# Attention in three units of 384 tokens instead of two batches of 576, with wider loads and first-matrix chunks cut by rows

## The chip, the cores and the metric

The kernel runs on one core of a Trainium2 chip. A core has five engines that run their own instruction queues in order and wait for each other by semaphores: TensorE (PE; its weight loads are listed as PEld), VectorE (DVE), ScalarE (ACT), GpSimd (POOL) and SyncE (SP), which here only issues transfers. The metric is the device time of one execution in microseconds. The kernel before took 690.56 us (median of 3 runs, 688.92 to 690.76).

## The reference

Local attention over 2 batches, 8 heads, 576 tokens and 64 columns a head, then two feed-forward blocks on the 1152 tokens of 512 columns:

```python
mask_plain = (rel >= 0) & (rel < 32)                          # heads 0 to 3
mask_dil = (rel >= 0) & (rel < 128) & (rel % 4 == 0)          # heads 4 to 7
scores = np.where(masks, scale * q @ k.T, -1e9)
attn = exp(scores - max); attn = attn / (sum + 1e-9)
x = (attn @ v), heads side by side                            # [1152, 512]

for e in range(4):                                            # experts, F = 1024
    out += p[:, e:e + 1] * (np.maximum(x @ w1[e], 0.0) @ w2[e])

h = out @ w_in                                                # 512 x 2048, float64
return (h - np.tanh(h)) @ w_out
```

`p` are the row-normalised domain probabilities. The second block's matrices come as float64.

## The kernel before, in words

**Feed-forward part.** The 1152 tokens are three groups g of 384 (T). The hidden columns are cut into 12 slices s of 512: 8 for the four experts, 4 for the tanh block. For one (s, g) there are seven *steps*: four h steps (`h_step`, 48 matmuls of 128x384, then a Relu or tanh on ACT and a subtraction on DVE that splits the result into a high and a low part) and three y steps (`y_step`, 36 matmuls of 128x512 and one eviction). Every product is three matmuls: high x high, high x low, low x high. Slices 0 and 1 are taken group by group, (0,0), (1,0), (0,1), (1,1), (0,2), (1,2); from slice 2 on each slice runs over all three groups.

**Weights.** A slice's weights are four chunks: c = 0, 1 from the first matrix, c = 2, 3 from the second. `w_load` fetches a chunk into one of three raw buffers; `w_split` copies it to the high part `whi` on ACT and writes the low part `wlo` on POOL (or DVE, for two of slice 0's chunks). Before, chunk c of the first matrix holds 256 hidden columns of all 512 rows. Slice 1's chunks are loaded at steps 0 to 3 and split at steps 1 to 4. In the tanh block `w_decode` on DVE first turns float64 into float32, in tiles of the tag "pn" of pool sp.

**Attention.** Two batches b; in each, a `Plain` object (heads 0 to 3) and a `Dilated` one (heads 4 to 7), each of two *pairs* of heads: pairs n = 0 to 3. A `Pair` has stages in *slots* 2n + lag: `scores` (PE, lag 0), `largest` of head a (mask, maximum on DVE, subtraction on POOL, lag 1 + a), `exps` (ACT, 1 + a), `norm` (sum and reciprocal on DVE, multiply on POOL, 2 + a), `p_transposes` (PE and a copy on ACT, 3 + a), `values` (PE, lag 5, then the high part of x on ACT and the low part on DVE). Scores of a head fill 5 stacks of 128 x 96. Within a slot the order is largest, norm, values, transposes, exps, early matmuls, splits, scores, loads. Values take two PSUM banks of pool "a" and transposes one or two; the pool has two banks.

**What sets the order.** All is written out by hand: each engine runs its instructions as the program emits them. Batch 0's 13 slots come first, with a few matmuls of step (0,0) put in as `early_h` when their x is there; then the steps run, and the table `beside` holds what is emitted after step i: loads, splits, decodes, and batch 1's slot t after step t (steps 0 to 12). Group 1 needs tokens of both batches. Transfers go through SP's queue alone, in the order of the program, and one that waits for a buffer holds those behind it.

Of the kernel before, what the change touches and what calls it, by code (L numbers as in the profile page):

```python
# [23 lines left out]
NST = 5  # L24
# [7 lines left out]
ROWS = S // DIL  # L32
CUTS = [(0, BQ), (BQ, BQ), (2 * BQ, ROWS - 2 * BQ)]

# [7 lines left out]
def _halves():  # L42


    out, at = [], [0, 0, 0]
    for b in range(2):
        for unit, plain in [((b, 0, ROWS), True)] + [((b, *cut), False) for cut in CUTS]:
            out.append((unit, plain, tuple(at)))
            nb, M, K = blocks(unit[2], plain)
            at[0] += 2 * nb * M  # L50
            at[1] += 2 * ((nb - 1) * (M if plain else K) + K)
            at[2] += nb * 4 * HEAD
    return out, at
# [6 lines left out]
def tile_local_attention_moe_tanhshrink(  # L60
# [30 lines left out]
    ld = ctx.enter_context(tc.tile_pool(name="ld", bufs=1))  # L91
# [14 lines left out]

    masks = {p: const.tile([128, NST, BK], F32, name=f"mask_{p}") for p in (True, False)}
# [5 lines left out]
    def emit_consts():  # L113

        mp, md = masks[True], masks[False]

        def band(out, m):
            nc.gpsimd.memset(out, 0.0)
            nc.gpsimd.affine_select(
                out=out, in_=out, pattern=[[1, BK]], base=-1, channel_multiplier=-1,  # L120
                compare_op=ALU.is_ge, fill=NEG,
            )
            nc.gpsimd.affine_select(
                out=out, in_=out, pattern=[[-1, BK]], base=HALO, channel_multiplier=1,
                compare_op=ALU.is_ge, fill=NEG,
            )

        def no_halo(out, in_):
            nc.gpsimd.affine_select(
                out=out, in_=in_, pattern=[[1, BK]], base=-HALO, channel_multiplier=0,  # L130
                compare_op=ALU.is_ge, fill=NEG,
            )

        for p in (0, BQ):
            band(mp[p:p + BQ, 1, :], BQ)
        no_halo(md[:, 0, :], mp[:, 1, :])
        nc.vector.tensor_copy(out=mp[:BQ, 0, :], in_=md[:BQ, 0, :])
        nc.vector.tensor_copy(out=mp[BQ:, 0, :], in_=mp[BQ:, 1, :])
        nc.vector.tensor_copy(
            out=mp[:, 2:, :], in_=mp[:, 1, :].unsqueeze(1).to_broadcast([128, NST - 2, BK])  # L140
        )
        make_identity(nc, ident)

    def emit_consts_dilated():
        mp, md = masks[True], masks[False]
        nc.gpsimd.tensor_copy(out=md[:, 1, :], in_=md[:, 0, :])
        nc.gpsimd.tensor_copy(out=md[:, 2:4, :], in_=mp[:, 1:3, :])
        for p in range(0, 128, 32):
            nc.vector.tensor_copy(out=md[p:p + 32, 4, :], in_=mp[:32, 1, :])
# [13 lines left out]
    class Plain:  # L163


        plain = True

        def __init__(self, b):
            self.b = b
            self.at = HALVES[b * (1 + len(CUTS))][2]  # L170
            self.q, self.k = {}, {}

        def load_qk(self, c):
            qo, ko, _ = self.at
            self.q[c] = ld.tile([128, S], F32, tag="q", name="pq", bufs=2)
            self.k[c] = ld.tile([128, S + HALO], F32, tag="k", name="pk", bufs=2)
            for src, o, n, dst in ((q, qo, S, self.q[c]), (k, ko, S + HALO, self.k[c])):
                nc.sync.dma_start(out=dst, in_=src[:, o + c * n:o + (c + 1) * n])

        def load_v(self):  # L180
            nb = S // BQ
            self.v = ld.tile([BK, nb, 4 * D], F32, tag="pv", name="pv")
            o = self.at[2]
            nc.sync.dma_start(
                out=self.v, in_=v[:BK, o:o + nb * 4 * D].rearrange("p (j f) -> p j f", j=nb)
            )

        def scores(self, c):

            out = []  # L190
            for j in range(2 * NST):
                o = min(j, S // BQ - 1) * BQ
                out.append((j % 2 * BQ, j // 2, self.q[c][:, o:o + BQ], self.k[c][:, o:o + BK]))
            return out

        def values(self):

            cut = S // BQ // 2
            return [
                (j, j * BQ, int(j >= cut), (j - cut * (j >= cut)) * BQ, BQ) for j in range(S // BQ)  # L200
            ]

        def spans(self, x):

            cut = S // BQ // 2 * BQ
            x = x[:, self.b * S:(self.b + 1) * S]
            return [(x[:, :cut], cut, None), (x[:, cut:], S - cut, None)]

    class Dilated:


        plain = False

        def __init__(self, b):
            self.b = b
            self.parts = HALVES[b * (1 + len(CUTS)) + 1:(b + 1) * (1 + len(CUTS))]
            self.q, self.k = {}, {}

        def load_qk(self, c):
            self.qat, self.kat, nq, nk = [], [], 0, 0  # L220
            for (_, _, W), _, _ in self.parts:
                self.qat.append(nq)
                self.kat.append(nk)
                nq, nk = nq + DIL * W, nk + DIL * (W + HALO)
            tail = BK - self.parts[-1][0][2] - HALO
            self.q[c] = ld.tile([128, S + 32], F32, tag="q", name="dq", bufs=2)
            self.k[c] = ld.tile([128, nk + tail], F32, tag="k", name="dk", bufs=2)
            nc.gpsimd.memset(self.q[c][:, nq:], 0.0)
            nc.gpsimd.memset(self.k[c][:, nk:], 0.0)
            for ((_, _, W), _, at), qo, ko in zip(self.parts, self.qat, self.kat):  # L230
                for src, o, n, dst, d in (
                    (q, at[0], DIL * W, self.q[c], qo),
                    (k, at[1], DIL * (W + HALO), self.k[c], ko),
                ):
                    nc.sync.dma_start(out=dst[:, d:d + n], in_=src[:, o + c * n:o + (c + 1) * n])  # L235

        def load_v(self):
            self.v = ld.tile([BK, DIL * len(CUTS), 4 * D], F32, tag="dv", name="dv")
            for u, (_, _, at) in enumerate(self.parts):
                n = DIL * 4 * D  # L240
                nc.sync.dma_start(
                    out=self.v[:, u * DIL:(u + 1) * DIL, :],
                    in_=v[:BK, at[2]:at[2] + n].rearrange("p (j f) -> p j f", j=DIL),
                )

        def scores(self, c):
            out = []
            for u, ((_, _, W), _, _) in enumerate(self.parts):
                for r in range(DIL):
                    o = self.qat[u] + r * W  # L250
                    w = self.kat[u] + r * (W + HALO)
                    full = W == BQ
                    out.append((
                        r % 2 * BQ if full else r * 32, 2 * u + r // 2 if full else NST - 1,
                        self.q[c][:, o:o + (BQ if full else 32)], self.k[c][:, w:w + BK],
                    ))
            return out

        def values(self):
            out = []  # L260
            for r in range(DIL):
                for u, ((_, p0, W), _, _) in enumerate(self.parts):
                    full = W == BQ
                    t = (2 * u + r // 2) * 128 + r % 2 * BQ if full else (NST - 1) * 128 + r * 32
                    out.append((u * DIL + r, t, r // 2, r % 2 * ROWS + p0, W))
            return out

        def spans(self, x):
            x = x[:, self.b * S:(self.b + 1) * S].rearrange("c (p r) -> c r p", r=DIL)
            return [(x[:, i:i + 2], 2 * ROWS, 2) for i in (0, 2)]  # L270

    class Pair:
# [7 lines left out]
        def scores(self):  # L280
            which = self.banks["s"]
            self.sb = [
                bank(which)[:, :NST * BK].rearrange("p (j c) -> p j c", c=BK) for _ in range(2)
            ]
            for part, j, qs, ks in self.h.scores(self.c):
                M = qs.shape[1]
                for a in range(2):
                    nc.tensor.matmul(  # L288
                        out=self.sb[a][part:part + M, j, :],
                        lhsT=qs[D * a:D * a + D, :], rhs=ks[D * a:D * a + D, :],  # L290
                        start=True, stop=True,
                    )

        def largest(self, a):
            s = sp.tile([128, 512], F32, tag="s", name="s")[:, :NST * BK].rearrange(
                "p (j c) -> p j c", c=BK
            )
            nc.vector.scalar_tensor_tensor(
# [453 lines left out]
```

## Time and profile before

| | us |
|---|---|
| median of 3 runs | 690.56 |
| the profiled execution | 689.82 |
| its span | 687.90 |
| TensorE busy | 652.1 (95%) |
| VectorE, ScalarE, GpSimd busy | 323.4, 205.1, 149.6 |

The span is the time from the first to the last instruction of the profile; the rest of the execution's time lies around it. The page's second part cuts the span into 40 slices of 17.2 us and gives the tenths of each that an engine was busy. TensorE's row begins 5767789 and is 9 from there to the last slice but one, so the idle time lies in the first seventh. The chain of work that ended last is 85% TensorE, and of it 40% in y steps and 42% in h steps.

### The profile page before, as it was taken

The page shows a single profiled execution, that of the slowest core. Times are in us where ns is not written, and L with a number is a line of the kernel's source. Part 1 is how long each engine was busy: PE and PEld are TensorE (multiplying, and loading weights), DVE is VectorE, ACT ScalarE, POOL GpSimd, SP SyncE. Part 2 cuts the span into 40 slices and gives each one's busy share as a digit, 9 for nine tenths or more (in the row PEclk, how much of TensorE's full clock was granted, in tenths as well). Part 3 has the DMA queues.
Part 4 walks back from the last instruction along what each step waited for, and adds up shares of the span by engine and source line. Part 5 has one row for each costly group of instructions (what it writes and reads, how often), then busy time and mean ns, then how long its engine had stood idle before and what let it go on. Part 6 is the DMA issues. An engine that isn't in the chain of part 4 may idle for free.

```text
span 687.9 us, 9361 instructions
## 1 busy us (share of the span) xinstructions
PE 652.1 (95%) x3839; PEld 580.4 (84%) x3839; DVE 323.4 (47%) x533; ACT 205.1 (30%) x376; POOL 149.6 (22%) x117
## 2 busy tenths in 40 slices
PE   5767789999999999999999999999999999999997
PEld 3556689999999999999999999888888888888886
DVE  6665442121222222222222222877687699698333
ACT  3453431214121121121121121333555443344221
POOL 4646410004221121121121121212022122122000
PEclk8698989999999999999999999999999999999999
DMA  9879100001221010010011021213133123220111
GB/s 250 222 142 263 31 1 1 1 0 55 70 68 55 31 61 32 31 61 31 31 61 31 31 62 30 92 61 92 38 100 98 47 96 94 70 99 7 47 46 46
DMA packets 27610, 46.23 MB, mean 67 GB/s; under 512 B 3504, under 2 KB 14512, under 8 KB 27376
## 3 DMA queue, kind: packets, MB, share of 16 engines
q1 hardware_dynamic: 27568, 45.64, 22.3%
q8 instruction: 30, 0.49, 0.3%
q14 instruction: 12, 0.10, 0.0%
HBM read 43.27 MB, written 2.36 MB: 66 GB/s over the span
## 4 chain that ended last, share of the span: by engine, by line
PE 85%; DVE 6%; DMA 3%; issue 2%; ACT 1%; POOL 1%; SPq 1%; DVEq 0%; POOLq 0%; ACTq 0%
PE bank_y L525 40%; PE bank_h L483 21%; PE bank_a L483 21%; DMA dk<-in_k_dram 2%; DMA raw<-in_moe_w_dram 1%; PE bank_a L335 1%; DVE t L433 1%; SPq L235 1%; POOL s L304 1%; PE bank_s L288 1%; DVE t L436 1%; DVE acc L537 1%; DVE t L429 1%; PE bank_y L670 1%; ACT h L494 1%
## 5 line engine op out<-in xcount | busy, mean ns | idle before, releaser
L525 PE MATMUL bank_y<-whi,h 128*128 128x512 f32 x864 | 277.5, 394 | 0.0
L525 PEld LDWEIGHTS bank_y<-whi,h 128*128 128x128 f32 x864 | 160.6, 188 | 39.1 <-DVE h L507 3.1
L525 PE MATMUL bank_y<-wlo,h 128*128 128x512 f32 x432 | 169.0, 391 | 0.0
L483 PE MATMUL bank_h<-x,whi 128*128 128x384 f32 x592 | 154.2, 341 | 0.0
L483 PE MATMUL bank_a<-x,whi 128*128 128x384 f32 x544 | 138.7, 335 | 2.6 <-DVE h L495 1.7
L459 POOL TENSOR_TENSOR wlo<-raw,whi 128x1024 fp32r<-128x1024 f32 x30 | 71.7, 2393 | 279.2 <-ACT whi L458 279.2
L483 PEld LDWEIGHTS bank_h<-x,whi 128*128 128x128 f32 x592 | 109.8, 192 | 3.0 <-issue 0.2
L483 PE MATMUL bank_h<-x,wlo 128*128 128x384 f32 x296 | 101.0, 341 | 0.0
L483 PEld LDWEIGHTS bank_a<-x,whi 128*128 128x128 f32 x544 | 98.0, 188 | 3.3 <-DVE h L495 2.2
L537 DVE SCALAR_TENSOR_TENSOR acc<-bank_y,pn,acc 128x512 f32<-128x512 f32 x63 | 47.1, 749 | 101.8 <-PE bank_y L525 101.8
L525 PEld LDWEIGHTS bank_y<-wlo,h 128*128 128x128 f32 x432 | 81.1, 188 | 15.4
L483 PE MATMUL bank_a<-x,wlo 128*128 128x384 f32 x272 | 90.9, 334 | 0.0
L494 ACT ACTIVATE h<-bank_h 128x384 fp32r<-128x384 f32 x50 | 24.5, 490 | 206.5 <-PE bank_h L483 206.5
L459 POOL TENSOR_TENSOR wlo<-t,whi 128x512 fp32r<-128x512 f32 x32 | 43.1, 1348 | 175.7 <-ACT whi L458 161.1
L495 DVE SCALAR_TENSOR_TENSOR h<-bank_h,h 128x384 fp32r<-128x384 f32 x50 | 27.8, 557 | 106.6 <-ACT h L494 106.6
L495 DVE SCALAR_TENSOR_TENSOR h<-bank_a,h 128x384 fp32r<-128x384 f32 x44 | 24.5, 558 | 69.0 <-ACT h L494 69.0
L483 PEld LDWEIGHTS bank_h<-x,wlo 128*128 128x128 f32 x296 | 56.8, 192 | 0.0
L483 PEld LDWEIGHTS bank_a<-x,wlo 128*128 128x128 f32 x272 | 51.1, 188 | 0.0
L494 ACT ACTIVATE h<-bank_a 128x384 fp32r<-128x384 f32 x44 | 21.6, 492 | 61.7 <-PE bank_a L483 61.7
L458 ACT ACTIVATE whi<-t 128x512 fp32r<-128x512 f32 x32 | 20.2, 630 | 57.8 <-DVE t L442 57.8
L458 ACT ACTIVATE whi<-raw 128x1024 fp32r<-128x1024 f32 x32 | 33.6, 1052 | 2.9 <-DMA raw<-in_moe_w_dram 2.9
L433 DVE SCALAR_TENSOR_TENSOR t<-raw,t 128x512 int32<-128x512 int32 x32 | 33.9, 1060 | 1.1
(163 smaller groups left out, 466.3 us busy)
## 6 DMA issues: line engine op xcount, KB each, us to landing
raw<-in_moe_w_dram SPq DMA_DIRECT2D x32, 512.0 KB, 3.6
raw<-in_moe_w_in_dram SPq DMA_DIRECT2D x16, 512.0 KB, 3.6
raw<-in_moe_w_out_dram SPq DMA_DIRECT2D x16, 512.0 KB, 3.3
dv<-in_v_dram SPq DMA_DIRECT2D x6, 384.0 KB, 8.2
out_dram<-oacc SPq DMA_DIRECT2D x8, 256.0 KB, 2.0
pv<-in_v_dram SPq DMA_DIRECT2D x2, 864.0 KB, 11.3
dk<-in_k_dram SPq DMA_DIRECT2D x8, 192.0 KB, 6.9
pk<-in_k_dram SPq DMA_DIRECT2D x4, 304.0 KB, 4.2
```

Of the source, the lines that this page charges most:

```text
L235: nc.sync.dma_start(out=dst[:, d:d + n], in_=src[:, o + c * n:o + (c + 1) * n])
L288: nc.tensor.matmul(out=self.sb[a][part:part + M, j, :], lhsT=qs[D * a:D * a + D, :], rhs=ks[D * a:D * a + D, :], start=True, stop=True,)
L304: nc.gpsimd.tensor_tensor(out=s, in0=s, in1=nm.unsqueeze(2).to_broadcast([128, NST, BK]), op=ALU.add)
L335: nc.tensor.transpose(pb[:BK, j * 128:(j + 1) * 128], self.p[a][:, j, :], ident)
L433: nc.vector.scalar_tensor_tensor(out=t, in0=high, scalar=-0x40000000, in1=t, op0=ALU.bitwise_and, op1=ALU.bitwise_or)
L458: nc.scalar.activation(out=hi, in_=raw, func=ACTF.Copy)
L459: (engine or nc.gpsimd).tensor_tensor(out=lo, in0=raw, in1=hi.bitcast(F32), op=ALU.subtract)
L483: nc.tensor.matmul(out=state["bank", f], lhsT=a, rhs=x[:, b_, :], start=(kk == 0 and n == 0), stop=(kk == KD - 1 and n == 2),)
L494: nc.scalar.activation(out=ht[:, 0, :], in_=hb, func=ACTF.Relu)
L495: nc.vector.scalar_tensor_tensor(out=ht[:, 1, :], in0=hb, scalar=0.0, in1=ht[:, 0, :].bitcast(F32), op0=ALU.max, op1=ALU.subtract,)
L525: nc.tensor.matmul(out=y, lhsT=a, rhs=b_, start=(f == 0 and n == 0), stop=(f == NF - 1 and n == 2),)
L537: nc.vector.scalar_tensor_tensor(out=acc[ch], in0=y, scalar=p, in1=acc[ch], op0=ALU.mult, op1=ALU.add)
```

## The change

Attention is cut by group instead of by batch: unit g holds the 384 tokens of group g (unit 1 is made of the end of batch 0 and the start of batch 1, two parts). Unit 0's slots come first; unit 1's slot t stands after step t and unit 2's slot t after step 14 + t, so that unit g is finished before group g's first step. A pair's scores are now 3 stacks of 96 (288 columns), or 4 of 80 (320) in unit 1's dilated pairs. Values take one PSUM bank and transposes one. Both pairs of a kind are loaded together, v on 128 partitions. The masks are small bf16 tiles for each unit, copied on DVE in slots 1, 9 and 10. Slice 0's splits stand in slots 4 (POOL), 7 (POOL), 9 (DVE) and 11 (POOL), before in slots 3 (DVE), 6 (POOL), 9 (DVE) and 11 (POOL). Slice 1's chunks are loaded at steps 0, 2, 4, 6 and split at steps 1, 3, 5, 7. A first-matrix chunk is 256 rows of all 512 columns, so every h step reads both chunks. The tag "pn" has two buffers, before three.

```diff
-ROWS = S // DIL
-CUTS = [(0, BQ), (BQ, BQ), (2 * BQ, ROWS - 2 * BQ)]
+UNITS = [[(0, 0, 96)], [(0, 96, 48), (1, 0, 48)], [(1, 48, 96)]]
...
+    def emit_mask(g, plain):
+        m = masks[g, plain]
+        copy = nc.vector.tensor_copy
+        if plain:
+            copy(out=cols(m, 0, 3), in_=wide(m_std, 3))
...
+        copy(out=cols(m, 0, 2), in_=wide(m_first if g == 0 else m_std, 2))
+        nc.vector.memset(m[:, 2 * BK:2 * BK + HALO], NEG)
         for p in range(0, 128, 32):
+            copy(out=m[p:p + 32, 2 * BK + HALO:3 * BK], in_=m_std[:32, :BQ])
...
         def values(self):
             h = self.h
-            xb = [bank(self.banks["x"]) for _ in range(2)]
-            for blk, t, i, o, n in h.values():
+            xb = bank(self.banks["x"])
+            for blk, keys, t, o, n in h.values():
...
+            (hi, src), (lo, _) = (h.order(xT[self.kk][:, j], xb) for j in range(2))
+            nc.scalar.activation(out=hi, in_=src, func=ACTF.Copy)
+            nc.vector.tensor_tensor(out=lo, in0=src, in1=hi.bitcast(F32), op=ALU.subtract)
...
-                dst = raw.rearrange("p (k f) -> p k f", k=KD)
-                src = a[:, c * 256:(c + 1) * 256].rearrange("(k p) f -> p k f", p=128)
+                dst = raw.rearrange("p (k f) -> p k f", k=2)
+                src = a[c * 256:(c + 1) * 256, :].rearrange("(k p) f -> p k f", p=128)
...
-        t = sp.tile([128, 512], F32, tag="pn", name="t", bufs=3).bitcast(I32)
+        t = sp.tile([128, 512], F32, tag="pn", name="t").bitcast(I32)
...
-        o = kk * 256 + (f % 2) * 128
-        return [t[:, o:o + 128] for t in wt[s, f // 2]]
+        o = kk % 2 * FV + f * 128
+        return [t[:, o:o + 128] for t in wt[s, kk // 2]]
...
+    for g in range(NG - 1):
+        put_load(g, 2, kinds[g + 1, True].load_qk)
+        put_load(g, 7, kinds[g + 1, True].load_v)
+        put_load(g, 6, kinds[g + 1, False].load_qk)
+        put_load(g, 11, kinds[g + 1, False].load_v)
+        put_load(g, 9, lambda g=g: emit_mask(g + 1, True))
+        put_load(g, 10, lambda g=g: emit_mask(g + 1, False))
+    put_load(0, 1, lambda: emit_mask(0, False))
...
-        (3, early[0], nc.vector), (6, early[1], nc.gpsimd), (9, early[2], nc.vector),
+        (4, early[0], nc.gpsimd), (7, early[1], nc.gpsimd), (9, early[2], nc.vector),
         (11, early[3], nc.gpsimd),
...
-        put(i, lambda sc=sc: w_load(*sc))
-        put(i + 1, lambda sc=sc: w_split(*sc))
+        put(2 * i, lambda sc=sc: w_load(*sc))
+        put(2 * i + 1, lambda sc=sc: w_split(*sc))
...
+    for g in range(1, NG):
+        for t, emits in enumerate(slots[g]):
+            for _, emit in sorted(emits, key=lambda e: e[0]):
+                put((g - 1) * 2 * PER + t, emit)
```

How the instructions stand in the queues, at three places. SP's queue at the start, before (pq, pk, pv are the plain heads' inputs, dq, dk, dv the dilated ones', raw a weight chunk):

```order
L178 DMA pq<-in_q_dram 128x576
L178 DMA pk<-in_k_dram 128x608
L178 DMA pq<-in_q_dram 128x576
L178 DMA pk<-in_k_dram 128x608
L418 DMA raw<-in_moe_w_dram 128x4x256
L184 DMA pv<-in_v_dram 96x2304
L418 DMA raw<-in_moe_w_dram 128x4x256
L235 DMA dq<-in_q_dram 128x256
L235 DMA dk<-in_k_dram 128x384
L235 DMA dq<-in_q_dram 128x256
L235 DMA dk<-in_k_dram 128x384
```

and after:

```order
L204 DMA q<-in_q_dram 128x384
L204 DMA k<-in_k_dram 128x416
L204 DMA q<-in_q_dram 128x384
L204 DMA k<-in_k_dram 128x416
L212 DMA v<-in_v_dram 128x1536
L204 DMA q<-in_q_dram 128x768
L204 DMA k<-in_k_dram 128x1024
L401 DMA raw<-in_moe_w_dram 128x2x512
L212 DMA v<-in_v_dram 128x1024
L401 DMA raw<-in_moe_w_dram 128x2x512 x2
```

The dilated pairs' q and k moved ahead of the first weight chunk, as two transfers for both pairs, and stand behind no buffer that has to come free.

POOL's queue in the first slots, before (s is the subtraction, pn__ the multiply of a head, wlo a split):

```order
L304 TENSOR_TENSOR s<-s,nm 128x480
L326 TENSOR_TENSOR pn__293<-p,rs 128x480
L304 TENSOR_TENSOR s<-s,nm 128x480
L326 TENSOR_TENSOR pn__349<-p,rs 128x480
L304 TENSOR_TENSOR s<-s,nm 128x480
L326 TENSOR_TENSOR pn__394<-p,rs 128x480
L459 TENSOR_TENSOR wlo<-raw,whi 128x1024
```

and after:

```order
L306 TENSOR_TENSOR s<-s,nm 128x288
L324 TENSOR_TENSOR pn__263<-p,rs 128x288
L449 TENSOR_TENSOR wlo<-raw,whi 128x1024
L306 TENSOR_TENSOR s<-s,nm 128x288
L324 TENSOR_TENSOR pn__307<-p,rs 128x288
L306 TENSOR_TENSOR s<-s,nm 128x288
L324 TENSOR_TENSOR pn__342<-p,rs 128x288
```

The first split on POOL moved from behind the fifth head's multiply (pn__394) to behind the third head's (pn__263).

TensorE's queue in a slot that holds values, beside the y steps, before (pt and last are the transposed weights of attention):

```order
L357 MATMUL bank_a<-pt,pv 64x64 x16
L357 MATMUL bank_a<-last,pv 64x64 x2
L335 MATMUL bank_a<-ident,pn__841 96x128 x4
L525 MATMUL bank_y<-whi,h 128x512
L525 MATMUL bank_y<-wlo,h 128x512
```

and after:

```order
L345 MATMUL bank_a<-pt,v 64x64 x12
L331 MATMUL bank_a<-ident,pn__692 96x128 x3
L515 MATMUL bank_y<-whi,h 128x512
L515 MATMUL bank_y<-wlo,h 128x512
```

The values' 18 matmuls into two banks became 12 into one; the transposes still stand right behind them.

## Rows read from the trace of the kernel before

**Rows 1.** Busy us by engine in four stretches; then clock, DMA share, GB/s.

```profile
0.00:43.90 43.90, 29.08 (x416) 21.11 (x416) 28.24 (x61) 19.46 (x34) 21.66 (x37) 0.81 0.88 220
43.90:109.53 65.63, 51.76 (x533) 44.58 (x533) 31.26 (x60) 23.33 (x43) 27.32 (x25) 0.90 0.32 91
109.53:142.62 33.09, 33.09 (x170) 30.20 (x169) 6.71 (x11) 6.01 (x11) 0.00 (x0) 1.00 0.00 1
142.62:687.90 545.28, 538.15 (x2725) 484.48 (x2723) 257.21 (x402) 156.28 (x288) 100.62 (x56) 1.00 0.18 56
```

**Rows 2.** The chain that ended last, 102 to 143 us (start us, us, what).

```profile
102.36 1.51 PE bank_a L357 x48
...
134.42 8.20 PE bank_y L525 x36
```

**Rows 3.** The same chain in the first 30 us.

```profile
4.83 1.06 PE bank_s L288 x40
...
7.30 11.29 DMA dk<-in_k_dram
...
19.65 0.67 PE bank_s L288 x16
...
27.84 1.26 PE bank_h L288 x48
```

**Rows 4.** TensorE's timeline, 52 to 85 us (in brackets: idle before, releaser).

```profile
52.85 1.87 PE L288 MATMUL bank_s<-pk,pq 64*64 64x96 f32 x38 [4.67 <-DVE s L298]
...
84.21 0.61 PE L335 MATMUL bank_a<-ident,pn__968 128*96 128x128 f32 x4 [3.00 <-DVE x L368]
```

**Rows 5.** Timeline of POOL and ACT, 47 to 55 us.

```profile
47.33 2.35 POOL L459 TENSOR_TENSOR wlo<-raw,whi 128x1024 fp32r<-128x1024 f32 x1 [1.23 <-ACT whi L458]
...
49.64 0.99 POOL L304 TENSOR_TENSOR s<-s,nm 128x480 f32<-128x480 f32 x1
...
51.17 0.47 ACT L494 ACTIVATE h<-bank_h 128x384 fp32r<-128x384 f32 x1
...
54.53 1.06 ACT L458 ACTIVATE whi<-raw 128x1024 fp32r<-128x1024 f32 x1 [2.89 <-DMA raw<-in_moe_w_dram]
```

**Rows 6.** Groups by line and form, 0 to 110 us (busy us, mean ns | idle).

```profile
L304 POOL TENSOR_TENSOR s<-s,nm 128x480 f32<-128x480 f32 x16 | 15.8, 988 | 21.7 <-DVE nm L303 21.5
L459 POOL TENSOR_TENSOR wlo<-raw,whi 128x1024 fp32r<-128x1024 f32 x6 | 14.2, 2372 | 14.2 <-ACT whi L458 14.2
L303 DVE TENSOR_REDUCE nm<-s 128x5 f32<-128x480 f32 x16 | 10.5, 654 | 0.6
...
L458 ACT ACTIVATE whi<-raw 128x1024 fp32r<-128x1024 f32 x8 | 8.4, 1051 | 2.9 <-DMA raw<-in_moe_w_dram 2.9
...
L298 DVE SCALAR_TENSOR_TENSOR s<-bank_s,mask_True 128x480 f32<-128x480 f32 x6 | 3.9, 645 | 1.1 <-PE bank_s L288 1.1
```

**Rows 7.** TensorE's timeline, 70 to 78 us: values, transposes, scores.

```profile
70.27 1.15 PE L357 MATMUL bank_a<-pt,pv 96*64 96x64 f32 x32
...
75.76 0.60 PE L335 MATMUL bank_a<-ident,pn__908 128*96 128x128 f32 x4
...
76.50 1.22 PE L288 MATMUL bank_s<-dk,dq 64*64 64x96 f32 x48
```

**Rows 8.** Timeline of DVE and POOL, 9 to 13 us.

```profile
9.64 0.17 DVE L320 TENSOR_SCALAR sm<-sm 128x5 f32<-128x5 f32 x1
...
11.42 0.99 POOL L304 TENSOR_TENSOR s<-s,nm 128x480 f32<-128x480 f32 x1
...
11.87 0.57 DVE L320 TENSOR_SCALAR sm<-sm 128x5 f32<-128x5 f32 x1
```

**Rows 9.** The page's second part: what the DMA engines moved, by slice.

```profile
GB/s 250 222 142 263 31 1 1 1 0 55 70 68 55 31 61 32 31 61 31 31 61 31 31 62 30 92 61 92 38 100 98 47 96 94 70 99 7 47 46 46
```

**Rows 10.** Timeline of POOL and DVE in the decode stage, 455 to 461 us.

```profile
455.63 1.29 POOL L459 TENSOR_TENSOR wlo<-t,whi 128x512 fp32r<-128x512 f32 x1 [9.13 <-ACT whi L458]
...
460.50 1.34 DVE L429 TENSOR_SCALAR t<-raw 128x512 int32<-128x512 int32 x1
```

More of the change, by code (lines that the diff above doesn't have):

```diff
@@ L45, in _halves @@
     out, at = [], [0, 0, 0]
[L46 to L52, printed above, removed]
+    for unit in UNITS:
+        for plain in (True, False):
+            for part in unit:
+                out.append((part, plain, tuple(at)))
+                nb, M, K = blocks(part[2], plain)
+                at[0] += 2 * nb * M
+                at[1] += 2 * ((nb - 1) * (M if plain else K) + K)
+                at[2] += nb * 4 * HEAD
     return out, at
@@ L209, in tile_local_attention_moe_tanhshrink @@
[L209 to L238, printed above, removed]
@@ L259, in values, with stacks @@
+            return out
+        def stacks(self):
+            if self.plain:
+                return [(j * BK, BK) for j in range(3)]
+            if self.short:
+                return [(j * self.K, self.K) for j in range(4)]
+            return [(0, 128), (BK, 128), (2 * BK - HALO, 128)]
         def values(self):
             out = []
[L261 to L265, printed above, removed]
@@ L266, in values @@
-            return out
-        def spans(self, x):
-            x = x[:, self.b * S:(self.b + 1) * S].rearrange("c (p r) -> c r p", r=DIL)
-            return [(x[:, i:i + 2], 2 * ROWS, 2) for i in (0, 2)]
+            for n in range(self.nb * len(self.parts)):
+                if self.plain or self.short:
+                    out.append((n, slice(0, self.width), n * BQ, n * self.M, self.M))
+                else:
+                    out.append((n, slice(0, BK), n * BQ, n * self.M, BQ))
+            if not self.plain and not self.short:
+                for n in range(self.nb):
+                    out.append((n, slice(BQ, 128), 256 + n * 32, n * self.M + BQ, 32))
@@ L280, in scores @@
         def scores(self):
[L281 to L286, printed above, removed]
+            self.sb = [bank(self.banks["s"]) for _ in range(2)]
+            for part, o, qs, ks in self.h.scores(self.c):
                 for a in range(2):
                     nc.tensor.matmul(
-                        out=self.sb[a][part:part + M, j, :],
+                        out=self.sb[a][part:part + qs.shape[1], o:o + ks.shape[1]],
                         lhsT=qs[D * a:D * a + D, :], rhs=ks[D * a:D * a + D, :],
```

295 lines of the change are left out of this document (146 added, 149 removed).

## The prediction

> **What bounds the kernel now.** I read the busy times first, cut at the points where the program's work changes [rows 1]: TensorE is busy for 538 of the last 545 us and for all of the 33.09 us before them, so from 109.5 us on nothing but matmul work can be won, and the change leaves that work alone. What can be won lies ahead of 109.5 us, where TensorE does only as much step work as in the 33.09 us that follow: two groups of seven steps (four h, three y), which on the chain end at 134.42 + 8.20 = 142.62 us [rows 2]. So the kernel before has four such groups behind it at 142.62 us, and after the change four must be done as well before the two programs are alike. I work out when.
>
> Before, the first stretch (attention of batch 0, with a little step work) lasts 43.90 us and the second (batch 1 beside 14 steps) 65.63 us [rows 1]. In the first the chain stands 11.29 us in one transfer of dk [rows 3]: pair 0's scores start at 4.83, pair 2's end only at 20.32, pair 3's at 29.10. In the second, step work is 33.09 - 3.1 = 30.0 us (18 matmuls of 174 ns, a 48th of (33.09 - 2 x 8.20) / 2 [rows 1, 2], run early both before and after). Attention on TensorE: scores 2 x 1.06 [rows 3] + 2 x 1.22 [rows 7] = 4.6; 40 transposes at 0.12 (six between 75.76 and 76.50 [rows 7]) = 4.9; values 2 x 36 x 36 ns [rows 7] + 2 x 1.51 [rows 2] = 5.6. That is 15.0, and 65.63 - 30.0 - 15.0 = 20.6 us is waiting and slower clock.
>
> **What makes the waiting.** Two kinds show in the timeline. Transposes that wait for the x of the values issued just ahead of them, since the values take two banks of a pool of two: 3.00 us the longest [rows 4]. And a chain through three queues: a split's wlo on POOL (2.35) stands ahead of the next subtraction on POOL, which stands ahead of the exp on ACT, which stands ahead of the next h's Relu at 51.17; DVE evicts a bank of scores behind that, and TensorE stood 4.67 us for it [rows 4, 5]. One split also waits 2.89 us on ACT for its chunk [rows 5].
>
> **The first stretch after.** A pair has 288 columns for 480 (320 in the short dilated case), so I scale by 0.6 (an estimate, as all durations of the new shapes here). DVE per slot: 0.645, 0.654 and the like sum to three ops of 0.39 [rows 6], plus two small ones at 0.17 to 0.57 [rows 8]: 1.5 to 2.3, I take 1.7. Pair 0's scores end at 4.83 + 24/40 of 1.06 = 5.5. Six small mask copies come in slot 1, 0.2 each by the small op's 0.17 [rows 8]: 1.2. Three slots, 5.1, to 11.8; then POOL's multiply 0.6 (0.988 x 0.6 [rows 6]), transposes 0.4, scores 32/48 of 1.22, 0.8 to 1.6 by the clock, 1.2: pair 2's scores end at 14.0, where 20.32 stood. The transfers must allow it: up to this pair's keys 2.52 MB are queued, and at the 250 GB/s of the first slice [rows 9] they are in at 10.1, the first weight chunk (3.05 MB) at 12.2. The two waits for dk go.
>
> From there a split takes their place. Chunk 0's split moves from slot 3 on DVE to slot 4 on POOL: from 13.2, ACT's half 1.05, POOL's 2.37 [rows 6], then behind it subtraction and multiply 0.6 each, transposes 0.5, six early matmuls 1.0 to 2.0, scores 1.0: pair 3 ends at 21 (before 29.10). From pair 3's scores to the steps it was 14.8. About eight attention ops lie on that way, 5.4 us x 0.4 = 2.2 less, and one x for two saves 1.1; against it the second POOL split comes a slot later, between pair 3's two heads, 1.2 of its 2.37, and DVE copies the next unit's masks, 0.8: 13.5. The first stretch ends at **34.5** (30 if the split's cover is better, 39 if only the 11.29 us transfer shrinks by half and nothing else).
>
> A rule bears on this. In the rows a DVE op that starts while POOL works ends with POOL's op: 11.87 + 0.57 = 12.44 against 11.42 + 0.99 = 12.41, while the same op took 0.17 alone [rows 8]. The Trainium skill (SBUF - State Buffer, "Who interferes with whom") says why: VectorE and GpSimd share a pair of ports as an exclusive lock, and whichever starts second fully blocks; a tensor_scalar, a copy or a cast can be such an op. The trace agrees. By that rule each POOL split could hold DVE's chain up to 2.37 us, which a kernel with one more of them in this stretch would pay; by the rows the held op's successor waits for POOL's own next op anyway, and I charge nothing. The rival below prices it.
>
> **Steps with unit 1.** Step work 30.0. Attention on TensorE: scores 2 x 0.64 + 2 x 0.81 = 2.9, 28 transposes 3.4, values (24 and 32 instructions for 36 and 48) 2 x 0.86 + 2 x 1.0 = 3.7: 10.0. Waits: values now take one bank, so the transposes' wait for x goes. The three-queue chain stays, since slice 1's splits stay on POOL ahead of the subtraction, only every second step now. Step 1's: Relu, 1.05, 2.37, 0.6, exp 0.4, Relu and the eviction of 0.5 and 0.4 against step 2's 2.1 us of matmuls, and the chunk is issued behind 1 MB of the next values, so it lands near 40 at 250 GB/s: 6.0. The splits of steps 3, 5 and 7 hold the transposes of the steps behind them: 1.05 + 2.37 + 0.6 + 0.6 = 4.6 from ACT's half to the multiply, against 2.7 of a y and 0.4 (1.5 late, twice) or 2.1 of an h and 0.6 (1.9). The first y waits 1.0 for the last h's rest, and a lower clock behind the longest stop costs 1.0 (the second stretch ran at 0.90 [rows 1]). Together **12.9**, bounds 6 (half of it hidden) and 20.6 (as before). End at 34.5 + 30.0 + 10.0 + 12.9 = 87.4.
>
> **Steps with unit 2** (14 steps that had no attention before). 33.1 + 9.5 (24 transposes, else the same) + waits. No split is there. Left are scores behind the eviction in step 2 of this unit, 2.2, the first y of either group 0.7 each, and a matmul's bank "a", which steps of this group share with attention, 1.1: about **5**, from 2 to the 20.6 of a whole second stretch. End at 135.0.
>
> **Edits costed at nothing.** Wider loads and row chunks: the byte count hardly moves, and past 110 us no chunk is waited for. First matrix by rows: an h step needs both chunks where it needed one, but they are split at least five steps ahead. Two pn buffers for three: the third decode of a row of three would wait for the first one's wlo; POOL has that done at 455.63 + 1.29 = 456.92 and DVE starts the third decode at 460.50 [rows 10], 3.6 us later. If that cover went, eight decodes would pay at most 1.3 each.
>
> **The sum.** 142.62 - 135.0 = 7.6 us less. The profiled execution took 689.82 (span 687.90, 1.9 around it); 689.82 - 7.6 = **682.2**. The median shown is 690.56, 0.7 above it; I keep 682.
>
> **Rivals.**
> - *The waits mostly go* (18%). If POOL is through its split before ACT needs it, the first stretch ends at 30, unit 1 waits 6, unit 2 waits 2: 31 + 30 + 10 + 6 + 33.1 + 9.5 + 2 = 121.6 with a spare 1 in the first term, so 21 less: 669. For it speaks that a split now comes every second step; against it that 2.37 us of POOL fit no h step of 2.1.
> - *The lock or a late load shows* (10%). POOL's splits in slots 4 and 7 hold DVE for 2.37 each and the mask copies for 1.2: 6 us of the 7.6 go, 688. For: rows 8. Against: who waits for DVE there waits for POOL too.
> - *Slower* (10%). Attention beside 28 steps in place of 14 pays the second stretch's 20.6 us twice: 34.5 + 40.0 + 20.6 + 42.6 + 20.6 = 158.3, 15.7 more than 142.62: 705.5. Its place is unit 2's steps; it decides once their waits exceed 5 + 7.6 = 12.6. For it: exp still stands ahead of the next Relu on ACT, and h steps of this group share bank "a" with attention. Against: the longest stops before had a split or a second x bank in them, and unit 2 has neither.
> - *The forecast* (62%), its own range 674 to 691 from the bounds of the three waits taken together.
>
> No change can be told from a change of under 0.3%, 2.1 us. The forecast gives 54 faster, 5 same, 3 slower; the first rival 18 faster; the second 5, 3 and 2; the third 10 slower: 0.77, 0.08, 0.15. The range goes from the first rival's 669, with 2 below it, to 692, where the third is left out.
>
> **What would show it.** Pair 2's scores should end near 14 and pair 3's near 21, with no wait for q or k; the first full h step should begin near 35. The longest stop of TensorE should lie in front of unit 1's second scores, 5 us or more, with a wlo of 2.4 us and a chunk's landing behind it. No transpose should wait for an x. Unit 2's 14 steps should take 46 to 49 us. From there on the same 545 us. It is wrong if unit 2 takes over 55 us, if the first stretch ends past 40, or if the decode stage shows TensorE stops that were not there.

## The result: 699 us, slower than before, and the profile after

The changed kernel takes 699.17 us (median of 4 runs, 697.82 to 701.66) against 690.05 for the kernel before beside it: a ratio of 1.0138 (95% interval 1.0103 to 1.0172). Forecast were 682 us and a gain, with a range to 692. The sign was wrong, and the time lies outside the range. The profiled execution took 699.97 us, its span is 698.20.

The same four stretches as in [rows 1], cut at the first scores of unit 1, the first step with unit 2, and the point where the four step groups are done (us busy on PE, PEld, DVE, ACT, POOL; then granted clock, DMA share, GB/s), and the chain of waits at that last point (start us, us, what):

```profile
0.00:41.83 41.83, 29.95 (x281) 19.31 (x281) 22.82 (x58) 14.77 (x26) 18.35 (x33) 0.76 0.59 194
41.83:99.14 57.31, 45.90 (x401) 38.93 (x401) 26.84 (x65) 19.07 (x35) 22.03 (x21) 0.88 0.38 123
99.14:153.18 54.04, 50.26 (x417) 41.19 (x417) 23.60 (x55) 15.28 (x31) 10.68 (x16) 0.97 0.03 12
153.18:698.20 545.02, 538.02 (x2724) 484.41 (x2723) 255.64 (x402) 156.11 (x288) 100.90 (x56) 1.00 0.18 56
```

```profile
153.18 4.18 PE bank_h L473 x24
```

The four groups are done at 153.18 us, where the kernel before had them at 142.62 [rows 1, 2]. That is 10.6 us later, and the span is 10.3 longer: the loss lies ahead of this point. Past it the two kernels agree (545.02 and 545.28 us), so whatever else the change did (row chunks, two pn buffers, wider loads) costs or brings nothing there.

| | forecast | after | after, scores grouped (below) |
|---|---|---|---|
| first stretch | 34.5 | 41.83 | 38.42 |
| unit 1's steps | 52.9 | 57.31 | 58.05 |
| unit 2's steps | 47.6 | 54.04 | 49.83 |

TensorE's timeline of the changed kernel shows the first surprise: the dilated scores of units 0 and 2 (start us, us, engine, line, operation, count, in brackets the idle time before and what ended it):

```profile
13.70 3.97 PE L284 MATMUL bank_s<-k,q 64*64 64x96 f32 x32
...
23.38 3.13 PE L284 MATMUL bank_h<-k,q 64*64 64x96 f32 x32
...
53.49 1.23 PE L284 MATMUL bank_s<-k,q 64*64 64x96 f32 x22 [5.73 <-DVE s L299]
...
64.56 0.78 PE L284 MATMUL bank_s<-k,q 64*64 64x80 f32 x32
...
108.79 0.72 PE L284 MATMUL bank_s<-k,q 64*64 64x96 f32 x22 [2.19 <-DVE s L299]
...
117.27 2.46 PE L284 MATMUL bank_s<-k,q 64*64 64x96 f32 x32
...
127.03 2.46 PE L284 MATMUL bank_s<-k,q 64*64 64x96 f32 x32
```

32 instructions take 2.46 us in unit 2 and 0.78 in unit 1, where all tiles are 64 wide; before, 48 took 1.22 [rows 7]. A single one lasts about as long here as in the kernel with grouped scores below (duration min/median/max in ns, here and there, for the two pairs of unit 2):

```profile
L284 PE MATMUL bank_s<-k,q x64: 242/255/293, 117.3 to 129.3; 64*64 64x96 f32 x32, 64*32 64x96 f32 x32
```

```profile
L286 PE MATMUL bank_s<-k,q x64: 242/243/293, 113.6 to 122.4; 64*64 64x96 f32 x32, 64*32 64x96 f32 x32
```

So what is lost is their overlap. What sets these pairs apart from those of the kernel before is their order. A token block of 96 queries is a 64-wide block and a 32-wide rest, and `Kind.scores` emits block, rest, block, rest. The kernel before emitted all blocks of 64 and then all rests of 32.

The longest stop of TensorE, 5.73 us, is at 53.49. Its chain, read on SP, ACT and POOL:

```profile
39.47 0.81 SPq L212 DMA_DIRECT2D v<-in_v_dram  x2
40.32 0.43 SPq L164 DMA_DIRECT2D pr<-in_moe_domain_probs_dram  x1
40.85 1.20 SPq L401 DMA_DIRECT2D raw<-in_moe_w_dram  x2
```

```profile
47.53 1.06 ACT L448 ACTIVATE whi<-raw 128x1024 fp32r<-128x1024 f32 x1 [2.93 <-DMA raw<-in_moe_w_dram]
```

```profile
48.66 2.34 POOL L449 TENSOR_TENSOR wlo<-raw,whi 128x1024 fp32r<-128x1024 f32 x1 [5.05 <-ACT whi L448]
50.96 0.67 POOL L306 TENSOR_TENSOR s<-s,nm 128x288 f32<-128x288 f32 x1
```

SP waits at unit 1's dilated v, whose buffer comes free with unit 0's last values; the probabilities and slice 1's first chunk are issued behind it. The chunk arrives at 47.5, and its split precedes the subtraction on POOL.

### The profile page after: what moved, and what is told of

It is laid out like the page before. It is cut to its first block, busy times and chain, and to the rows that moved or that the text cites. A ratio compares the mean times of both kernels' runs of the same rounds, so it can differ in the third digit from the quotient of the medians.

```text
span 698.2 us, 9399 instructions
## 1 busy us (share of the span) xinstructions
PE 664.1 (95%) x3819; PEld 583.8 (84%) x3819; DVE 328.9 (47%) x580; ACT 205.2 (29%) x380; POOL 152.0 (22%) x125
## 4 chain that ended last, share of the span: by engine, by line
PE 87%; DVE 6%; issue 2%; POOL 2%; ACT 2%; DMA 1%; SPq 0%; DVEq 0%; POOLq 0%; ACTq 0%
PE bank_y L515 40%; PE bank_h L473 20%; PE bank_a L473 20%; PE bank_s L284 2%; PE bank_a L345 1%; PE bank_a L331 1%; DMA raw<-in_moe_w_dram 1%; DVE t L416 1%; ACT h L484 1%; DVE s L299 1%; PE bank_y L662 1%; DVE t L419 1%; DVE acc L527 1%; DVE t L412 1%; POOL s L306 1%
## 5 line engine op out<-in xcount | busy, mean ns | idle before, releaser
L449 POOL TENSOR_TENSOR wlo<-raw,whi 128x1024 fp32r<-128x1024 f32 x31 | 74.1, 2393 | 254.4 <-ACT whi L448 254.4
```

The lines of the kernel that those rows point to most:

```text
L449: (engine or nc.gpsimd).tensor_tensor(out=lo, in0=raw, in1=hi.bitcast(F32), op=ALU.subtract)
```

## The experiments

Times are medians beside the kernel before on the same chip; intervals (95%) are of the ratio to it. The runs stand on several chips, on which the kernel before took 689.9 to 690.7 us, so a difference of under 1 us between two of them says nothing.

| run | us | ratio to before |
|---|---|---|
| e_grouped | 694.30 | 1.0036 to 1.0080 |
| e_disjoint | 698.92 | 1.0094 to 1.0154 |
| e_before_mixed | 696.84 | 1.0064 to 1.0138 |
| e_load_early | 699.26 | 1.0102 to 1.0174 |
| e_grp_load | 692.78 | 1.0015 to 1.0059 |
| e_grp_both | 690.99 | 1.0005 to 1.0055 |
| e_grp_warm | 693.85 | 1.0038 to 1.0082 |
| e_grp_all | 688.15 | 0.9948 to 0.9992 |
| e_split_last | 683.65 | 0.9894 to 0.9927 |
| e_undo_cut | 697.50 | 1.0064 to 1.0126 |
| e_before_all | 693.03 | 1.0027 to 1.0062 |
| e_best_mixed | 690.55 | 0.9973 to 1.0020 |
| e_best_two | 685.33 | 0.9887 to 0.9948 |

**The order of the scores.** Two theories: a change between 64-column and 32-column tiles makes TensorE run dry (A), or a rest waits because it uses columns of the block in flight just ahead (B; in the changed kernel four of the seven neighbours in a pair share columns, in e_disjoint one). Rival: narrow matmuls are slow as such.

```diff
+            if not self.plain and not self.short:
+                out = out[::2] + out[1::2]            # e_grouped
...                                                    # or, in its place:
+                out = [out[i] for i in (0, 5, 4, 7, 2, 1, 6, 3)]   # e_disjoint
```

> The changed kernel with the 64-wide score matmuls of a dilated pair of units 0 and 2 first and their 32-wide rests after them, as the kernel before had its own; nothing else moves. Theory A (each change between 64-column and 32-column tiles makes TensorE run dry, eight of them in a pair): the two pairs of unit 2 fall from 2.46 us each to 0.8 to 0.9, those of unit 0 from 3.97 and 3.13 to 1.0 to 1.6; the mark of the four step groups falls by 6 to 11 us from 153.2, the run to 688 to 693. Theory B (a rest waits because its columns lie under the block just in front of it): the same, since most neighbours are then apart. Rival C (32-wide or 96-column matmuls are slow by themselves, whatever stands between them): the pairs stay over 2.2 us and the run within 2 us of 699.

> The changed kernel with a 64-wide block and a 32-wide rest still taking turns, seven changes in a pair, but each rest is taken from a block of the other half of the columns, so that six of the seven neighbours share no columns (four of seven shared none in the changed kernel or fewer). Theory A (the change of width itself empties TensorE): unit 2's pairs stay at 2.2 to 2.6 us and the run at 697 to 701. Theory B (the shared columns): unit 2's pairs fall to 0.9 to 1.3 us and the run to 689 to 694.

Unit 2's pairs in the kernel with grouped scores, then in the one with other columns:

```profile
113.57 0.89 PE L286 MATMUL bank_s<-k,q 64*64 64x96 f32 x32
121.73 0.89 PE L286 MATMUL bank_s<-k,q 64*64 64x96 f32 x32
```

```profile
116.12 2.46 PE L286 MATMUL bank_s<-k,q 64*64 64x96 f32 x32
125.87 2.46 PE L286 MATMUL bank_s<-k,q 64*64 64x96 f32 x32
```

The same 32 instructions take 0.89 us with one change of width and 2.46 with seven, whichever columns they use. B and the rival fall, and A stands: each change costs. (The changes in a pair of the changed kernel are seven; the first expectation says eight.) The run with grouped scores gained 4.9 us, less than expected. It is still slower than the kernel before, by 4.4 us, so the order is not all of the miss. Its first three stretches:

```profile
0.00:38.42 38.42, 26.20 (x280) 17.68 (x280) 23.84 (x58) 14.71 (x26) 18.64 (x33) 0.76 0.64 216
38.42:96.47 58.05, 48.09 (x401) 40.81 (x401) 26.81 (x65) 19.08 (x35) 21.61 (x21) 0.86 0.36 119
96.47:146.30 49.83, 45.52 (x418) 38.20 (x417) 23.58 (x55) 15.05 (x31) 10.67 (x16) 1.00 0.03 12
```

In the kernel before, the same mixing (two blocks, one rest):

```diff
+            full, rest = out[:2 * DIL], out[2 * DIL:]
+            out = []
+            for i, r in enumerate(rest):
+                out += [full[2 * i], r, full[2 * i + 1]]
```

> The kernel before with its dilated scores put into turns, two 64-wide blocks to one 32-wide rest, eight changes of width in a pair where it had one; nothing else moves. Theory A at the 0.2 us a change that unit 2 of the changed kernel shows ((2.46 - 0.8) / 8): a pair at full clock takes 2.6 to 3.0 us where it took 1.22, and the four pairs together add 6 to 9 us, the run at 695 to 700 against 690. Theory B (four of the eight neighbours share columns, as in the changed kernel): about the same. Rival C (the widths themselves): no change, within 1.5 us of 690.

```profile
84.40 2.82 PE L292 MATMUL bank_s<-dk,dq 64*64 64x96 f32 x48
```

2.82 us for 1.22 [rows 7], with eight changes for one, 0.23 us each, and 7 us in the run: the order by itself makes the old kernel about as slow as the new one.

**The late chunk and the clock.** First the chunk alone, in the changed kernel:

```diff
+    put_load(0, 8, lambda: w_load(*early[4]))
     for i, sc in enumerate(early[4:]):
-        put(2 * i, lambda sc=sc: w_load(*sc))
+        if i > 0:
+            put(2 * i, lambda sc=sc: w_load(*sc))
```

> The changed kernel with one DMA moved: slice 1's first chunk is issued at slot 8 of the first stretch, ahead of unit 1's dilated v, where it was issued in step 0 at 40.85. Theory: the stop of 5.73 us in front of unit 1's second scores is the chain of that late load (ACT's split at 47.53 after 2.93 us for the DMA, POOL's split to 51.0, s, DVE): it falls by 2 to 3.5 us to 2.3 to 3.8, and the run to 695 to 698. Rival: VectorE, which waits 3.92 us for the probabilities' load and then works until 47.8, and POOL's 2.34 us split keep the stop at 4.5 or more, and the run falls by 1 us or less.

```profile
53.83 1.23 PE L284 MATMUL bank_s<-k,q 64*64 64x96 f32 x22 [2.86 <-DVE s L299]
```

The stop halved, and the time did not move. The profiled execution is the slowest of the four (702.30; the others took 698.88 to 699.28), and its first stretch was 3.1 us longer than the changed kernel's. These are 10 to 25, 25 to 41 and 41 to 60 us of the changed kernel and then of this one; behind the five busy times stands the granted clock:

```profile
10.00:25.00 15.00, 12.26 (x88) 7.74 (x90) 7.91 (x22) 5.08 (x11) 8.35 (x10) 0.50 0.65 233
25.00:41.00 16.00, 10.92 (x133) 8.32 (x131) 10.03 (x21) 7.48 (x12) 5.73 (x7) 0.89 0.42 121
41.00:60.00 19.00, 12.52 (x84) 11.04 (x85) 5.70 (x17) 4.59 (x9) 6.66 (x5) 0.64 0.54 172
```

```profile
25.00:41.00 16.00, 14.51 (x120) 10.97 (x118) 7.78 (x20) 5.86 (x10) 5.72 (x7) 0.50 0.47 149
```

TensorE ran at the lower level (0.50, 1.2 GHz) from 25 to 41 us. That goes with the slow execution; why the other three did not gain is not shown. So on top of grouped scores I tried the chunk with an earlier split, the probabilities' DMA, and zero matmuls in TensorE's waits, apart and together:

```diff
+    slots[0][12].append((6, lambda: w_split(*early[4])))      # e_grp_load, with the load above
...
+                nc.sync.dma_start(out=pr, ...)                 # e_grp_both: behind slot 4
...
+            if self.h.g == 0:                                  # e_grp_warm: ahead of transposes
+                fill(pb, 8 if (self.kk, a) == (0, 0) else 3)
...
+            if (self.h.g, self.kk) == (1, 1):                  # and of unit 1's second scores
+                fill(bank("a"), 10)
```

> The kernel with grouped scores, and slice 1's first chunk issued at slot 8 of the first stretch and split at slot 12, both ahead of unit 1's dilated v; nothing else moves. Theory P (the stop in front of unit 1's second scores, 4.54 us in the kernel with grouped scores, comes of that chunk: its landing and POOL's split ahead of POOL's subtraction): the stop falls to 1 to 2.5 us and the time by 2 to 4 us from 694.3, to 690 to 692.5. Theory C (what is saved there is given back, because the stretch from 35 to 60 us runs at TensorE's lower clock, as the first try with this chunk showed: stop 2.86 us, same time): the stop falls and the time stays at 693 to 695.

> As the kernel with grouped scores and the earlier chunk, and the DMA of the probabilities issued after slot 4, where it stood behind unit 1's dilated v (VectorE waits 3.79 us for it at 41.2 with two of unit 1's h and its first scores behind). Theory P: VectorE's wait goes, the stop falls below 1.5 us, the time to 688.5 to 691.5. Theory C: within 1 us of the run without the earlier probabilities.

> The kernel with grouped scores, and zero matmuls (bf16, 128 x 512, results overwritten) ahead of the transposes of the first stretch (8 in front of the first, 3 in front of the others) and 10 ahead of unit 1's second scores, where TensorE waits; nothing of the computation changes. Theory C (the lower clock after those stops costs about 3 us in 38 to 44 and 3 us in 49 to 55 us): the granted clock stays at 0.9 to 1.0 from 25 to 60 us, the stops stay in length, and the time falls by 3 to 8 us, to 686 to 691. Rival (the chain through VectorE, POOL and ScalarE sets these stretches, whatever TensorE's clock is): the clock rises and the time stays at 692 to 696; or the filler delays the transposes, up to 700.

> All of these together: grouped scores, earlier chunk and probabilities, zero matmuls in the waits. Theory P with theory C: the two gains add, 684 to 689, which would be faster than the kernel before (690). If only one of them holds, 688 to 692; if the filler costs TensorE time once the stops are gone, 692 to 697.

The stop in front of unit 1's second scores in the kernels with grouped scores, with the earlier chunk, with the filler alone, and with all together:

```profile
49.37 1.23 PE L286 MATMUL bank_s<-k,q 64*64 64x96 f32 x22 [4.54 <-DVE s L301]
```

```profile
47.79 1.23 PE L286 MATMUL bank_s<-k,q 64*64 64x96 f32 x22 [2.66 <-DVE s L301]
```

```profile
48.23 1.23 PE L295 MATMUL bank_s<-k,q 64*64 64x96 f32 x22 [6.37 <-DVE s L310]
```

```profile
45.30 0.72 PE L294 MATMUL bank_s<-k,q 64*64 64x96 f32 x22 [2.55 <-DVE s L309]
```

And the first stretches of the filler alone:

```profile
0.00:35.84 35.84, 25.67 (x309) 15.79 (x309) 22.50 (x59) 14.73 (x26) 18.22 (x33) 1.00 0.68 227
35.84:94.61 58.77, 46.94 (x411) 38.69 (x411) 26.81 (x65) 19.06 (x35) 22.03 (x21) 0.91 0.35 120
```

In this execution (691.19, the fastest of the eight) the clock stays at 1.00 through the first stretch, which ends 2.6 us sooner (35.84 for 38.42), but the stop grows from 4.54 to 6.37, with 2.33 us of filler ahead of it: ScalarE still waits 4.45 us there for the chunk, and the time stays (693.85). The ten executions with the probabilities lie at 689.2 to 691.2 (clock 0.975 to 0.978) and at 694.6 to 695.0 (0.966), so their median says little. By means, with twice their standard error, the chunk alone gives 1.6 ± 1.5 us, with the probabilities 2.3 ± 1.9, the filler alone 0.3 ± 1.6, and all together 6.2 ± 1.7. The filler, which shows nothing by itself, gives 3.9 ± 2.2 on top of the chunk and the probabilities; how the rest is shared is inside the scatter.

**The splits behind the attention.** Three stops of unit 1 were left, each behind a split.

```diff
-            put(2 * i + 1, lambda sc=sc: w_split(*sc))
...                                      # behind the loop that puts unit 1's and 2's slots:
+    for i, sc in enumerate(early[5:]):
+        put(2 * i + 3, lambda sc=sc: w_split(*sc))
```

> The kernel with everything together (688.15 us), and the splits of slice 1's second to fourth chunks issued last in their steps, behind the subtraction and normalisation of unit 1 that they stood ahead of on POOL and ScalarE; nothing else moves. Theory P (POOL's 2.4 us split is what the transposes of unit 1 wait for: stops of 2.14, 1.44 and 1.85 us, each right behind a split at 51.40, 62.59 and 71.46): the three stops fall to 0 to 0.5 us each, the time by 3 to 5 us, to 683 to 685.5. Rival (a split then holds up the next step's subtraction instead, or its chunk comes late for the first products of slice 1): stops of the same size in other places, 686.5 to 690.

TensorE's waits on POOL there, in the kernel with everything together, and with the splits last:

```profile
55.08 0.53 PE L343 MATMUL bank_a<-ident,pn__697 128*96 128x128 f32 x3 [2.14 <-POOL pn__697 L334]
...
66.35 0.53 PE L343 MATMUL bank_a<-ident,pn__791 128*96 128x128 f32 x3 [1.44 <-POOL pn__791 L334]
...
75.26 0.63 PE L343 MATMUL bank_a<-ident,pn__905 128*80 128x128 f32 x4 [1.85 <-POOL pn__905 L334]
```

```profile
53.48 0.54 PE L343 MATMUL bank_a<-ident,pn__693 128*96 128x128 f32 x3 [0.81 <-POOL pn__693 L334]
...
69.14 0.63 PE L343 MATMUL bank_a<-ident,pn__901 128*80 128x128 f32 x4 [0.59 <-POOL pn__901 L334]
```

5.4 us of waits became 1.7 (a third, 0.33, is not shown), and the run fell by 4.5, as expected. At 683.65 us this kernel beats both the kernel before and the changed one.

**What it is not.** The parts that were costed at nothing, undone in the kernel with grouped scores; and the three additions put into the kernel before.

```diff
-                src = a[c * 256:(c + 1) * 256, :].rearrange("(k p) f -> p k f", p=128)
+                src = a[:, c * 256:(c + 1) * 256].rearrange("(k p) f -> p k f", p=128)
...
-            pn_ = sp.tile([128, 512], F32, tag="pn", name="pn_")
+            pn_ = sp.tile([128, 512], F32, tag="pn", name="pn_", bufs=3)
```

> The kernel with grouped scores (694.3 us), with the first-matrix chunks cut by columns again and three buffers for pn again, as the kernel before had them. The prediction costed both at nothing: 693.5 to 695, no change. Rival (rows hold the first products of each slice up, or two pn buffers hold POOL): 690 to 693, with fewer waits past 150 us. Second rival (the rows' longer runs in DRAM did help the loads): slower, 695.5 to 698.

```profile
25.00:41.00 16.00, 13.34 (x103) 10.38 (x106) 7.17 (x18) 7.79 (x13) 6.64 (x7) 0.50 0.46 151
...
150.85:695.80 544.95, 538.03 (x2725) 484.40 (x2723) 257.35 (x402) 156.11 (x288) 100.71 (x56) 1.00 0.18 56
```

Past the four groups it takes 544.95 us, as with row chunks and two buffers (545.10): that part of the question is settled. The time of the whole was higher than expected, 697.5, and goes in part with the clock: its profiled execution stood at 0.50 from 25 to 41 us (the first row), three of its four executions had a mean clock of 0.963 to 0.968 and took 697.4 to 698.1, one had 0.975 and took 692.75, like the kernel with grouped scores at that clock (692.8 to 693.1). At 0.968, though, it took 697.37 where the kernel with grouped scores took 694.97 and 695.25. The loads themselves were no slower: the eight chunks issued in the first 60 us landed 6.7 us after their issue (median of the profiled execution), with row chunks 7.0. Whether column chunks or the third buffer make the lower clock likelier in the first 50 us, and what the rest is, stays open.

> The kernel before with the same three additions that brought the changed one to 688.15: slice 1's first chunk issued at slot 9 and split at slot 12, the probabilities' DMA after slot 6, and zero matmuls in TensorE's waits. If the gain is due to what both kernels share (the late chunk, the late probabilities, the lower clock after stops): it falls by 3 to 6 us from 690.3, to 684 to 687. If these waits were made by the change: within 1.5 us of 690.3.

The kernel before does not gain; it loses 3.1 us. The stop in front of its second scores fell from 4.67 [rows 4] to 1.28, but a new one of 5.05 stands behind it, and ahead of that ScalarE waits for slice 1's second chunk, which SP issues behind six transfers of dilated q and k:

```profile
62.41 1.09 PE L345 MATMUL bank_a<-ident,pn__760 128*96 128x128 f32 x4 [5.05 <-POOL dq L227]
```

```profile
56.99 1.06 ACT L468 ACTIVATE whi<-raw 128x1024 fp32r<-128x1024 f32 x1 [4.18 <-DMA raw<-in_moe_w_dram]
```

The additions don't carry over as they stand. The run does not show what a version fitted to the old queue would bring.

**How much the order costs where nothing else is late.** The fastest kernel with its scores in turns again, and with two blocks, two rests, two blocks, two rests:

```diff
-                out = out[::2] + out[1::2]
+                out = [out[i] for i in (0, 2, 1, 3, 4, 6, 5, 7)]   # e_best_two; e_best_mixed: neither
```

> The fastest kernel so far (683.65 us) with the dilated scores of units 0 and 2 in turns again, as in the changed kernel, seven changes of width in a pair where it has one. Theory A (each change empties TensorE): unit 2's pairs take 2.46 us again, unit 0's 3 to 4; with what waits behind them 5 to 9 us, the run at 688.5 to 692.5. If their cost in the changed kernel came mostly through its late chunk and its low clock: 685 to 687.

> The fastest kernel so far with two blocks, two rests, two blocks, two rests: three changes in a pair. Theory A at 0.26 us a change ((2.46 - 0.89) / 6): unit 2's pairs at 1.3 to 1.5 us, the run at 684.5 to 687. If the first change costs and the others do not, or the other way round, the pairs are at 0.9 or at 2.2 us and more.

```profile
104.61 1.32 PE L294 MATMUL bank_s<-k,q 64*64 64x96 f32 x32
113.21 1.32 PE L294 MATMUL bank_s<-k,q 64*64 64x96 f32 x32
```

A pair takes 0.89, 1.32 and 2.46 us with 1, 3 and 7 changes: 0.22 and 0.29 us a change. The runs take 683.65, 685.33 and 690.55. The first two cannot be told apart (their intervals overlap); the third is clear of both. Of the 6.9 us between the first and the third, the direct price in four pairs is some 5.7 (2.46 for 1.42 and 0.89 in unit 0, 2.46 for 0.89 twice in unit 2); but the profiled execution, one of five at 687.8 to 688.9, has its four groups done at 141.12, only 3.8 us after the fastest kernel's 137.31, so part of the price does not show there. The other five took 692.2 to 693.2 at a lower mean clock (0.985 for 0.990 to 0.993). What tips an execution from one to the other was not tried.

## Why the prediction was wrong

*Where the bound lies.* Right: all that changed lies ahead of the four groups' end, and the 545 us behind it stayed.

*The dilated scores.* This step failed. The prediction priced them by count, "scores 32/48 of 1.22", 0.81 at full clock and 1.2 in the first stretch. They took 2.46 in unit 2 and 3.97 and 3.13 in unit 0. Nothing was wrong with the count: the row of before was of instructions in another order, and the order is what the changed `scores` function altered. The diff showed it (the rest is appended inside the loop over blocks) and I read it as the same work. The Trainium skill has a rule that would have warned of it (TensorEngine Tiling (Array Packing), "Key Properties"): a change of the tiling mode, not just of the tile, drains TensorE. The trace agrees: 0.89 us with one change, 2.46 with seven, on the same or on other columns. Grouping takes 6.9 us off the four groups' end in the profiled executions (146.30 for 153.18) and 4.9 off the median. It is the largest single term of the miss that a run shows, but not enough to turn the sign: with it undone the kernel still took 694.30 against 689.86 beside it.

*The other attention terms on TensorE.* Each unit was priced at 9.5 to 10.0. In unit 2 of the kernel with grouped scores, at full clock, its scores, transposes and values keep TensorE busy for these times (one row each: the stretch, busy us and count, clock, DMA share, GB/s):

```profile
96.47:146.30 49.83, 3.60 (x112) 1.00 0.03 12
```

```profile
96.47:146.30 49.83, 4.15 (x24) 1.00 0.03 12
```

```profile
96.47:146.30 49.83, 4.38 (x112) 1.00 0.03 12
```

That is 12.1 for the 9.5 forecast (2.9, 2.9, 3.7). A share of a longer row is too little for a shorter group: three transposes took 0.49 to 0.55 us there and four 0.60 to 0.64 in unit 1, where 0.12 apiece was forecast; 24 scores took 0.73 for the 0.64 of the share, and 32 values of a dilated pair 1.27 for 1.0. It is 2.6 us too little in unit 2, and about as much in unit 1 (42.65 busy in the fastest kernel without its filler, 44.98 - 2.33, for 40.0):

```profile
38.20:85.96 47.76, 44.98 (x411) 37.18 (x411) 29.43 (x64) 18.46 (x35) 21.90 (x21) 0.97 0.39 134
```

*The first stretch.* Forecast 34.5, bounds to 39; measured 41.83, past the 40 that the prediction gave as a sign of being wrong. Pair 2's scores ended at 17.7 for 14.0 and pair 3's at 26.5 for 21. The waits for dk went as forecast; one of 2.73 us for a plain k stayed, ahead of pair 1. Of the 7.3 us, 3.4 go with the order of the scores (38.42), another 2.6 with the clock (35.84 with it at 1.00, one profiled execution). The prediction allowed for the lower clock in the scores and in six early matmuls alone; it stood at 0.50 from 10 to 25 us, as in the kernel before.

*Unit 1.* The waits were right, and no transpose waits for an x: 11.4 us idle (57.31 - 45.90) for 11.9 forecast without the clock, and the stop of 5.73 for "5 us or more", with the chunk 5.7 us after the stretch began, as forecast. What failed is the lower clock, priced at 1.0: the granted clock was 0.88, and TensorE was busy 3.3 us more than in the fastest kernel (45.90 for 42.65, at 0.97).

*Unit 2.* The waits were overpriced by 1.2 (3.8 idle for 5, the stop of 2.19 as forecast). The 6.4 us missing, 7.6 without that, are the scores (6.75 us in the unit for 3.60, so 3.1), the shapes (2.6 to 2.9) and a clock of 0.97 (about 1.6, what is left). The slower rival had this unit as its place, but its mechanism, waits over 12.6 us, did not come; the loss was TensorE's own work.

*The lock.* DVE's small op at 30.29 took 1.97 us beside POOL's split at 29.86 and ended with it (32.26 and 32.23), as the Trainium skill's rule has it (SBUF - State Buffer, "Who interferes with whom"):

```profile
30.29 1.97 DVE L320 TENSOR_SCALAR sm<-sm 128x3 f32<-128x3 f32 x1
```

```profile
29.86 2.37 POOL L449 TENSOR_TENSOR wlo<-raw,whi 128x1024 fp32r<-128x1024 f32 x1 [0.45 <-ACT whi L448]
```

Charging nothing for it was not tested by itself; what a run does show is the price of where unit 1's splits stand on POOL's queue (4.5 us in the run with the splits last).

*Summed:* 18.2 us lie between 135.0 and 153.18. Grouping the scores brings back 6.9, the shapes are some 5 (2.6 in each of units 1 and 2), the clock is 2.6 + 2.3 + 1.6 = 6.5 by the terms above, and the waits of units 1 and 2 were 1.7 fewer than forecast. That makes 16.7; but the clock's 1.6 in unit 2 is also in the 6.9, since that clock was 1.00 in the profiled execution with grouped scores. So some 15 us are accounted for, and 3 were not taken apart. Of these terms the order of the scores is shown by experiment; the shapes and the clock are read from busy times of one execution each.

## What to carry to other kernels

Price a group of matmuls by a row with the same order of tile shapes, not only the same count; where a loop emits tiles of two widths in turns, sort it by width first. A stretch that runs into TensorE's waits can lose twice, by the wait and by a lower clock behind it, and taking one limit away may show nothing until the other is gone: try the two together before either is dropped. On a queue shared by splits and a dependent chain, put the work that nobody waits for yet behind the chain.

## What was not expected of the hardware

A change between 64-column and 32-column tiles cost 0.22 to 0.29 us at the full clock. Unit 0's pairs, at a clock of 0.50 most of the time, took 3.97 and 3.13 us for 1.42 and 1.20. A stop was not always followed by the lower level: behind the stop of 2.19 us in unit 2 the changed kernel's clock was 0.57 from 110 to 113 us, and behind one of the same length the kernel with grouped scores had 1.00 from 104 to 120. In the lower-clock stretches the same program's executions came apart by up to 6 us (689.2 to 695.0 with the earlier chunk and probabilities), while the fastest kernel's lie within 0.7 (683.42 to 684.10). The eleven zero matmuls that both kernels start with were followed by a clock of 0.50 from 10 to 20 us in the changed kernel; with TensorE's later waits filled as well it stood at 1.00 to 40 us in one profiled execution, and at 0.77 to 0.89 from 10 to 25 us in two others that had the same filler.
